# A decode layer on one core: projections as rows through four column tiles, K loads in pairs, and an attention loop without a prologue

## The chip, the cores and the metric

The kernel runs on one core of one Trainium2 chip, the chip's other cores idle. The metric is the device time of one execution in microseconds (us), the median of several runs.

In the text PE is the tensor engine, DVE the vector engine, ACT the scalar engine and "the stream" is the sequence of loads from device memory into on-chip memory. A "slot" is one of ten on-chip buffers of 16 KB a partition (2 MB) into which all large loads go.

## The reference

One token passes through one transformer layer: modulation from a condition vector, attention with 32 query heads over a cache of 4 heads x 65,536 keys, then a gated feed-forward.

```python
def reference(A_x, A_k_cache, A_v_cache, A_wq, A_wo, B_x, B_w_gate, B_w_up, B_w_down, c, w_mod):
    mod = (silu(c) @ w_mod)                 # 1024 -> 6 x 1024: sa, ca, ga, sb, cb, gb
    h = layernorm(x) * (1 + ca) + sa
    x = x + ga * attention(h)               # wq 1024x4096, caches 4x65536x128, wo 4096x1024
    h = layernorm(x) * (1 + cb) + sb
    x = x + gb * ((gelu(h @ w_gate) * (h @ w_up)) @ w_down)   # F = 3584
    return x
```

All weights and caches are bf16. The bytes are w_mod 12.6 MB, wq 8.4, the caches 134.2, wo 8.4, gate, up and w_down 7.3 each: 185.6 MB, each byte used once.

## The kernel before

The parts that the change touches. Loads are planned in the order in which they are issued, and a load waits until the previous job in its slot has been used:

```python
        wmod_v = w_mod.rearrange("(k p) n -> p k n", p=P)
        wq_v = A_wq.rearrange("(k p) n -> p k n", p=P)
        wo_v = A_wo.rearrange("(p k) n -> p k n", p=P)
        wg_v = B_w_gate.rearrange("(k p) n -> p k n", p=P)
        # ... cut
        for i in range(NC + 2):
            if i < NC:
                j_k[i] = plan_load(kv_src(kh, i), kv_view, i % SITES, kfill[i % SITES])
            if i >= 2:
                j = i - 2
                j_v[j] = plan_load(kv_src(vh, j), kv_view, SITES + j % SITES, vfill[j % SITES])
        tail = iter([8, 9, 0, 1, 2, 4, 3, 5, 6, 7, 8, 9] + [0, 1, 2, 4, 3, 5, 6, 7])
        j_o = [(plan_load(wo_v[:, k:k + 8, :], flat(8, D), next(tail)), k, 8) for k in range(0, HQ, 8)]
        # ... gate, up, w_down the same way
```

Each projection keeps a 128x128 tile of the weights stationary and streams one column, the vector. The result comes out as a column and needs no turning:

```python
                for kk in range(nk):
                    for j in range(nblk):
                        w = pick(view, kk, j) if pick else view[:, kk, j * P:(j + 1) * P]
                        ins = pe.matmul(
                            bank[:, j:j + 1], w, rhs[:, k0 + kk:k0 + kk + 1],
                            start=first, stop=True, skip_group_check=True,
                        )
```

The attention goes through 32 chunks of 64 keys a partition (2 MB of K and 2 MB of V each). PE transposes a K chunk, multiplies it with q, DVE and ACT do the softmax pieces, and PE multiplies with V two steps later (called PV). Four steps are written out, the other 28 run in a loop of four steps:

```python
        for i in range(FIRST):
            pe_step(i)
            others_step(i)
        with nc.Fori(it0, it1, engines=OrderedEngineSet([pe.engine]), head_slot={pe.engine: 0}) as it:
            # ... cut
```

Ahead of the ten slots a number of small tensors are allocated; in this kernel the slots begin at byte 62,208 of each partition.

## Time and profile before

| | before |
|---|---|
| median time | 442.9 us (442.8 to 443.1) |
| span of the profiled run | 441.7 us |
| loaded | 186.08 MB, of which 185.61 by the load queue |
| load queue's share of the 16 DMA engines | 98.8% |
| PE busy | 75% |

The page of the kernel before: first the busy time of each engine, then the DMA queues with packets, MB and share of the 16 engines' span.

```profile
PE 332.8 (75%) x7849; PEld 322.9 (73%) x7849; DVE 164.9 (37%) x282; ACT 143.1 (32%) x548; POOL 3.8 (1%) x21
...
DMA packets 15537, 186.08 MB, mean 421 GB/s; under 512 B 1553, under 2 KB 1553, under 8 KB 3985
...
q1 hardware_dynamic: 15472, 185.61, 98.8%
q8 instruction: 25, 0.41, 0.3%
```

The number to read is 98.8%: the engines that load are hardly ever idle between the first and the last load. The windows view of the same kernel says it stretch by stretch. Its columns are the stretch, then busy time and count of each engine, then the granted PE clock, the DMA share and GB/s.

```profile
5.00:60.00 55.00, 20.91 (x657) 19.92 (x658) 2.24 (x15) 0.18 (x1) 0.56 (x1) 1.00 1.01 427
60.00:110.00 50.00, 43.93 (x963) 42.28 (x962) 27.38 (x36) 20.58 (x70) 0.00 (x0) 0.91 1.01 428
110.00:360.00 250.00, 226.47 (x5006) 221.38 (x5007) 123.83 (x191) 113.36 (x442) 0.00 (x0) 0.80 1.01 431
360.00:433.00 73.00, 37.94 (x1128) 36.28 (x1124) 10.67 (x37) 7.65 (x35) 0.56 (x1) 0.53 1.01 425
```

427, 428, 431, 425 GB/s: no stretch has a gap. The Trainium skill, "DMA: Bandwidth & Descriptors", section "Where 436 GB/s comes from", gives 435.2 GB/s as the ceiling of the fabric; this trace lies 1 to 2% below it. So the time is about the bytes over the rate, plus about 2 us before the stream runs and 5.3 us after it. The end of the stream is read from the timeline of PE (start, duration, line, instruction group; in brackets how long the engine idled and what ended it):

```profile
417.37 2.02 PE L316 MATMUL kt_ps<-h_col,slot 128*128 128x1 bf16 x56 [2.31 <-DMA slot<-in_B_w_up_dram]
421.62 2.02 PE L316 MATMUL kt_ps<-h_col,slot 128*128 128x1 bf16 x56 [2.23 <-DMA slot<-in_B_w_up_dram]
426.71 1.84 PE L316 MATMUL kt_ps<-u_col,slot 128*128 128x1 bf16 x64 [3.06 <-DMA slot<-in_B_w_down_dram]
431.48 1.87 PE L316 MATMUL kt_ps<-u_col,slot 128*128 128x1 bf16 x64 [2.93 <-DMA slot<-in_B_w_down_dram]
436.37 2.86 PE L316 MATMUL kt_ps<-u_col,slot 128*128 128x1 bf16 x96 [3.02 <-DMA slot<-in_B_w_down_dram]
```

Each block costs about 2 us of matmuls and is waited for 2.2 to 3.1 us. PE would be done long before the data.

### The profile page before, as it was taken

Reading aid. Unit: us, or ns where it says so; the run is one execution under the profiler, and the core shown is the slowest. Engines: PE = TensorE matmul, PEld = TensorE weight load, DVE = VectorE, ACT = ScalarE, POOL = GpSimd, SP = SyncE. Lnnn points to the kernel's source line nnn. Section 1 sums busy time; section 2 is a strip of 40 time slices with the busy share of each in tenths; the row PEclk is TensorE's granted clock in tenths of the full one; section 3 lists DMA queues with packets and bytes.
Section 4 is the critical chain, followed back from the end, with each engine's and each line's share of the span. In section 5 each row is a group of like instructions: output and inputs, shape, how many; then the busy total and the mean of one; then the engine's idle time right before and its main releaser. Section 6 shows DMA issues by size and latency. Waiting matters only on the chain.

```text
span 441.7 us, 16769 instructions
## 1 busy us (share of the span) xinstructions
PE 332.8 (75%) x7849; PEld 322.9 (73%) x7849; DVE 164.9 (37%) x282; ACT 143.1 (32%) x548; POOL 3.8 (1%) x21
## 2 busy tenths in 40 slices
PE   2333468888989898898899898897989894463534
PEld 1333468878989798798898798787989794463534
DVE  1000036544545455444536445364454442310000
ACT  1000014444554344455443346353435353000000
POOL 2000000000000000000000000000000000000000
PEclk9999999987768969777959869699597785555555
DMA  8999999999999999999999999999999999999995
GB/s 330 428 423 426 437 427 429 426 430 422 432 426 432 432 433 429 430 429 435 430 433 430 430 429 434 429 433 431 430 429 435 428 435 429 420 424 425 426 425 213
DMA packets 15537, 186.08 MB, mean 421 GB/s; under 512 B 1553, under 2 KB 1553, under 8 KB 3985
## 3 DMA queue, kind: packets, MB, share of 16 engines
q1 hardware_dynamic: 15472, 185.61, 98.8%
q8 instruction: 25, 0.41, 0.3%
q14 instruction: 8, 0.06, 0.0%
q10 hardware_dynamic: 32, 0.00, 0.0%
HBM read 185.60 MB, written 0.00 MB: 420 GB/s over the span
## 4 chain that ended last, share of the span: by engine, by line
DMA 81%; PE 17%; issue 1%; SPq 1%; DVE 0%
DMA slot<-in_A_v_cache_dram 53%; DMA slot<-in_B_w_gate_dram 9%; PE kt_ps L417 9%; DMA slot<-in_A_k_cache_dram 8%; DMA slot<-in_B_w_down_dram 7%; DMA slot<-in_w_mod_dram 5%; PE b L481 4%; PE sc_ps L437 3%; PE kt_ps L316 1%; SPq L212 1%; PE b L451 0%; PE b L461 0%; DVE kt_sb L516 0%; PE b L668 0%; DVE y_row L670 0%
## 5 line engine op out<-in xcount | busy, mean ns | idle before, releaser
L417 PE MATMUL kt_ps<-ident,slot 128*128 128x128 bf16 x2048 | 170.1, 250 | 6.9 <-DMA slot<-in_A_k_cache_dram 3.2
L516 DVE COPY kt_sb<-kt_ps 128x2048 bf16<-128x2048 bf16 x96 | 117.6, 1225 | 102.2 <-PE kt_ps L417 102.1
L417 PEld LDWEIGHTS kt_ps<-ident,slot 128*128 128x128 bf16 x2048 | 147.5, 114 | 8.6 <-issue 7.2
L516 ACT ACTIVATE kt_sb<-kt_ps 128x2048 bf16<-128x2048 bf16 x32 | 60.1, 1877 | 219.9 <-PE kt_ps L417 219.9
L481 PE MATMUL b<-p_sb,slot 128*128 128x8 bf16 x2048 | 71.0, 167 | 29.4 <-DMA slot<-in_A_v_cache_dram 22.5
L481 PEld LDWEIGHTS b<-p_sb,slot 128*128 128x128 bf16 x2048 | 65.0, 100 | 32.2 <-DMA slot<-in_A_v_cache_dram 23.9
L547 ACT ACTIVATE p_sb<-sc_ps,mneg 128x64 bf16<-128x64 f32 x256 | 83.6, 560 | 4.2 <-DVE mneg L542 4.2
L547 ACT ACTIVATION_READ_ACCUMULATOR p_sb<-sc_ps,mneg 128x1 f32 x256 | 77.2, 364 | 0.0
L437 PE MATMUL sc_ps<-q_buf,kt_sb 128*128 128x8 bf16 x2048 | 67.1, 167 | 1.1 <-issue 1.1
L437 PEld LDWEIGHTS sc_ps<-q_buf,kt_sb 128*128 128x128 bf16 x2048 | 64.3, 99 | 1.3 <-issue 1.2
L316 PE MATMUL kt_ps<-h_col,slot 128*128 128x1 bf16 x448 | 16.2, 172 | 16.2 <-DMA slot<-in_B_w_up_dram 9.1
L316 PEld LDWEIGHTS kt_ps<-h_col,slot 128*128 128x128 bf16 x448 | 15.5, 118 | 16.9 <-DMA slot<-in_B_w_up_dram 9.5
L535 DVE TENSOR_REDUCE m_col<-sc_ps 128x8 f32<-128x512 f32 x32 | 21.8, 681 | 4.4 <-PE sc_ps L437 4.4
L316 PE MATMUL sc_ps<-s_col,slot 128*128 128x1 bf16 x384 | 11.5, 165 | 15.7 <-DMA slot<-in_w_mod_dram 15.7
L316 PEld LDWEIGHTS sc_ps<-s_col,slot 128*128 128x128 bf16 x384 | 11.0, 105 | 16.3 <-DMA slot<-in_w_mod_dram 16.3
L540 DVE TENSOR_REDUCE mg<-b 8x1 f32<-8x128 f32 x32 | 8.9, 279 | 34.8 <-PE b L451 34.8
L316 PE MATMUL sc_ps<-h_col,slot 128*128 128x1 bf16 x256 | 7.4, 165 | 12.5 <-DMA slot<-in_A_wq_dram 12.5
L316 PEld LDWEIGHTS sc_ps<-h_col,slot 128*128 128x128 bf16 x256 | 7.1, 104 | 12.8 <-DMA slot<-in_A_wq_dram 9.2
L461 PE MATMUL b<-negi,mg 8*128 8x8 f32 x64 | 14.8, 301 | 0.4 <-DVE mg L540 0.4
L461 PEld LDWEIGHTS b<-negi,mg 8*128 8x128 f32 x64 | 11.8, 229 | 2.7 <-DVE mg L540 0.6
L316 PE MATMUL kt_ps<-u_col,slot 128*128 128x1 bf16 x224 | 6.6, 165 | 9.0 <-DMA slot<-in_B_w_down_dram 9.0
L316 PEld LDWEIGHTS kt_ps<-u_col,slot 128*128 128x128 bf16 x224 | 6.3, 104 | 9.3 <-DMA slot<-in_B_w_down_dram 6.1
(74 smaller groups left out, 62.9 us busy)
## 6 DMA issues: line engine op xcount, KB each, us to landing
slot<-in_A_k_cache_dram SPq DMA_DIRECT2D x32, 2048.0 KB, 29.5
slot<-in_A_v_cache_dram SPq DMA_DIRECT2D x32, 2048.0 KB, 33.3
slot<-in_w_mod_dram SPq DMA_DIRECT2D x8, 1536.0 KB, 18.9
slot<-in_A_wq_dram SPq DMA_DIRECT2D x4, 2048.0 KB, 37.2
slot<-in_A_wo_dram SPq DMA_DIRECT2D x4, 2048.0 KB, 36.7
slot<-in_B_w_gate_dram SPq DMA_DIRECT2D x4, 1792.0 KB, 39.1
slot<-in_B_w_up_dram SPq DMA_DIRECT2D x4, 1792.0 KB, 29.1
slot<-in_B_w_down_dram SPq DMA_DIRECT2D x3, 2048.0 KB, 30.2
```

What stands on the lines that cost most here:

```text
L212: sp.dma_start(j.view, j.src).then_inc(j.tok[0], 16)
L316: ins = pe.matmul(bank[:, j:j + 1], w, rhs[:, k0 + kk:k0 + kk + 1], start=first, stop=True, skip_group_check=True,)
L417: ins = pe.transpose(kt_ps[:, half * 2048 + t * P:half * 2048 + (t + 1) * P], j_k[i].view[:, b * TB + t, :], ident[:, :],)
L437: ins = pe.matmul(sc_ps[:, base + n * REP:base + (n + 1) * REP], kt_sb[:, j % 2, n, :], q_buf[:, j % SITES, :], start=True, stop=True,)
L461: ins = pe.matmul(b6[:, 256:256 + REP], mg8[:, j % 2:j % 2 + 1].to_broadcast([REP, P]), negi[:, :], start=True, stop=True,)
L481: ins = pe.matmul(b7[:, s * REP:(s + 1) * REP], j_v[j].view[:, n, :], p_sb[:, s, n, :], start=(n == 0), stop=(n == CH - 1),)
L516: ev[i % SITES][b].done(act.activation(dst, src, ACT.Copy) if E_ is AC else dve.tensor_copy(dst, src))
L535: m1[s].done(dve.tensor_reduce(m_col[:, j % 2, :].unsqueeze(2), scv, AX.X, ALU.max))
L540: m2[s].done(dve.tensor_reduce(mg8[:, j % 2:j % 2 + 1], b6[0:REP, 32:32 + P], AX.X, ALU.max))
L547: ins = act.activation(p_sb[:, s, :, h], scv[:, h, :], ACT.Exp, bias=mneg[:, j, h:h + 1], scale=scale, accum_out=z_all[:, j, h:h + 1],)
```

## The change

The intent is to take work off PE and to make loads longer. Five things change together:

1. All projections but w_down keep the vector stationary, padded to 32 columns of which one is used, and stream rows of 512 weights. Four such matmuls use the four column tiles of the PE array. The results come out as rows, which are copied, turned by f32 transposes and gathered.
2. The weights' rows are split over partitions so that both rows of a wq, gate or up block are contiguous, and K is loaded two chunks at a time: packets of 32 KB for K, 16 for wq, 14 for gate and up, in place of 16, 8 and 7.
3. Half of wo is loaded early, after the fourth K chunk, into slots that were idle during the attention.
4. c and x are loaded with eight elements a partition (c in place of its load by rows, x in addition to it): two loads of 128 packets of 16 bytes.
5. The loop starts at step 0, with semaphores counted up in advance and zeroed tiles for the steps that do not exist.

```diff
+KU = 2
+ROW = 512
+QD = 32
...
+        act.dma_start(c_in[:, :], c[0].rearrange("(p k) -> p k", p=P)).then_inc(c_sem, 16)
+        act.dma_start(x_in[:, :], A_x[0, 0].rearrange("(p k) -> p k", p=P)).then_inc(x_sem, 16)
...
-        wq_v = A_wq.rearrange("(k p) n -> p k n", p=P)
+        wq_v = A_wq.rearrange("(p k) n -> p k n", p=P)
...
+            if i == SITES:
+                j_o = [plan_o(k) for k in range(0, 16, 8)]
+            if i < NC and i % KU == 0:
+                j_k[i] = plan_load(kv_src(kh, i, KU), flat(KU * CH, DH), i % SITES, kfill[i % SITES // KU], KU)
...
+        def row_matvec(place, jobs, pad, ready, last_k, between=None):
...
+                    for out, c0 in place(k):
+                        ins = pe.matmul(
+                            out, pad[:, k, :], jb.view[:, kk, c0:c0 + ROW],
+                            start=k <= last_k[0], stop=k >= last_k[1], skip_group_check=True,
+                        )
...
+        def quad(bank, g):
+            return kt_fp[QD * g:QD * (g + 1), bank * ROW:(bank + 1) * ROW]
...
+            for i, a in enumerate(cols):
+                ins = pe.transpose(dst[:, i * w:i * w + n], src[:, a], identf[0:src.shape[0], 0:n])
...
-        for i in range(FIRST):
-            pe_step(i)
-            others_step(i)
...
+        with nc.Fori(0, NC // SITES, engines=OrderedEngineSet([pe.engine]), head_slot={pe.engine: 0}) as it:
...
-    slots = [nc.alloc_sbuf_tensor(f"slot{i}", [P, SLOT], dt.bfloat16) for i in range(NSLOT)]
+    slot_all = nc.alloc_sbuf_tensor("slots", [P, NSLOT * SLOT], dt.bfloat16)
+    slots = [slot_all[:, i * SLOT:(i + 1) * SLOT] for i in range(NSLOT)]
```

Because other small tensors are now allocated ahead of them, the slots begin at byte 65,088 in place of 62,208. Nothing in the diff says so.

## The prediction

> **What bounds the kernel now.** The DMA stream. The page gives 186.08 MB over a 441.7 us span and the load queue 98.8% of the 16 engines' time. The windows view shows 420 to 449 GB/s in almost every stretch from 5 to 433 us (429 to 432 GB/s in the attention), never a gap. The Trainium skill ("DMA: Bandwidth & Descriptors", "Where 436 GB/s comes from") puts the fabric at 435.2 GB/s; this trace is within 1 to 2% of it. Outside the stream lie about 2 us at the start and 5.3 us at the end (timeline: 96 last matmuls from 436.37, then short steps and the store).
>
> PE is busy 75% but follows the data: the waits view charges 22.5 us to V loads, and each w_gate or w_up block takes 2.0 us of matmuls in a 4.3 us arrival interval.
>
> **What the change does.**
> 1. PE: the one-column matmuls of the mod, q, wo, gate and up projections (384+256+256+448, about 30 to 36 ns each in the timeline) become 336 matmuls of 512 columns on four column tiles. The trace has no such matmul. From the transposes (128 columns in 57 ns warm, 108 cold) I estimate 0.22 us warm, 0.43 cold each; four overlapping give about 5 us for gate, 5 for up, 9 for wo. The skill ("TensorE: Matmul & The Clock Gate", "Part 3: Packing small matmuls") reports 2.38x for three column tiles; no run here shows it yet. Saves some 6 us, off the critical path.
> 2. Added: evacuating rows (about 0.65 us), eight f32 turns (about 0.25 us each, from the trace's f32 weight load), gathers: about 3 us after wo, gate and up each, so 9 to 10 us of serial chain.
> 3. Loads: K in 4 MB pairs (32 KB a row), wq, gate and up with both rows contiguous. wq blocks land 4.90 us apart, KV blocks of equal size 4.86: about 5 ns a packet, so about 1.1 us saved. Fewer instructions to fetch (-0.4 us), two small loads of 128 tiny packets each (+0.6 us).
> 4. Half of wo (4.2 MB, 9.8 us of stream) moves ahead of the fifth K chunk. The attention therefore ends about 12 to 15 us later (before: last PV 374.3; expected 386 to 389).
>
> **Critical path.** From the last PV the serial chain is about 6.6 (combine) + 9 (wo) + 3 + 3.3 (norm) + 5 + 3 + 5 + 3 + 6.7 (w_down) + 2.4 = 47 us, so 435 at the earliest, against the stream's end at about 436 plus 5.3. Some 6 us of slack are left where there were some 17. The time stays that of the bytes.
>
> **Prediction: 442.0 us, 80% range 439.5 to 446.5.** Faster by over 2%: 1%; within 2%: 90%; slower: 9%.
>
> **Right if:** bytes unchanged, stream at 425 to 433 GB/s to about 434 us, last w_down block at about 435 and still waited for by PE; last PV at 386 to 389; K interval slightly shorter.
>
> **Wrong if:** column tiles don't overlap (gate and up then 12 us or more each at a cold clock: the chain passes the stream and the end comes at 450 to 461); DMA share drops below 0.95 after 400 us because w_down's slots come free late; K pairs leave too few loads queued and gaps appear in the attention; or 32 KB packets run nearer 435 GB/s (then 438 to 440).

## The result, and the profile after

The changed kernel takes 443.4 us (443.3 to 443.6, six runs) against 442.9 (442.8 to 443.1, six runs). The ratio is 1.0011, interval 0.9998 to 1.0024: the same time. Ratios in this text are the mean time of one kernel's fast runs over that of the other's in the same rounds, so not quite the ratio of the medians quoted. Their intervals are about 0.13% either way, some 0.6 us: a difference smaller than that, between kernels timed on different chips, is weak evidence by itself.

| | before | after |
|---|---|---|
| median time | 442.9 us | 443.4 us |
| loaded | 186.08 MB | 185.89 MB |
| packets of the load queue | 15,472 | 11,632 |
| last w_down wait ends | 436.37 us | 436.66 us |
| last PV ends | 374.3 us | 389.3 us |
| PE instructions | 7,849 | 7,107 |

The lines of the page after that answer to those above:

```profile
PE 351.4 (80%) x7107; PEld 316.9 (72%) x7107; DVE 176.2 (40%) x300; ACT 146.5 (33%) x553; POOL 11.7 (3%) x25
...
DMA packets 11957, 185.89 MB, mean 421 GB/s; under 512 B 1568, under 2 KB 1568, under 8 KB 1952
...
q1 hardware_dynamic: 11632, 185.61, 98.7%
q8 instruction: 13, 0.21, 0.2%
```

The same bytes, a quarter fewer packets, half the instruction fetches, and the queue is as full as before. PE's busy time did not fall: 351.4 us against 332.8, at a mean granted clock of 0.740 against 0.789. By this measure the intent to take work off PE was not met; PE does not set the time here. The windows of the changed kernel:

```profile
5.00:60.00 55.00, 28.31 (x203) 11.69 (x203) 10.40 (x24) 1.71 (x3) 7.27 (x2) 0.64 1.01 427
60.00:110.00 50.00, 42.69 (x907) 41.97 (x907) 21.07 (x26) 15.15 (x52) 0.00 (x0) 0.74 1.00 426
110.00:360.00 250.00, 229.15 (x5014) 223.99 (x5010) 124.03 (x194) 114.00 (x441) 0.00 (x0) 0.78 1.00 430
360.00:433.00 73.00, 47.41 (x876) 36.00 (x877) 19.90 (x54) 14.28 (x59) 0.55 (x1) 0.68 1.01 424
```

The stream was to be slightly faster in the attention, where K comes in packets twice as long. It is 430 in place of 431 GB/s. The prediction held as a whole, but a gain of about one microsecond that it counted on is not there. The timeline of PE after shows the last PV (before, it ran from 372.46 for 1.84 us), the projections and the end:

```profile
387.49 1.85 PE L625 MATMUL b<-p_sb,slots 128*128 128x8 bf16 x64 [2.96 <-ACT p_sb L691]
...
396.28 5.30 PE L392 MATMUL kt_ps<-slots,o_pad 128*32 128x512 bf16 x64 [0.39 <-DVE o_pad L766]
...
402.40 1.16 PE L453 MATMUL sc_ps<-identf,kt_sb 128*128 128x128 f32 x8 [0.82 <-DVE kt_sb L774]
...
406.94 5.08 PE L392 MATMUL kt_ps<-slots,h_pad 128*32 128x512 bf16 x56 [1.10 <-DVE h_pad L447]
...
417.45 1.04 PE L392 MATMUL kt_ps<-slots,h_pad 128*32 128x512 bf16 x14 [1.60 <-DMA slots<-in_B_w_up_dram]
421.76 1.89 PE L392 MATMUL kt_ps<-slots,h_pad 128*32 128x512 bf16 x14 [3.26 <-DMA slots<-in_B_w_up_dram]
...
426.82 1.85 PE L372 MATMUL b<-u_col,slots 128*128 128x1 bf16 x64 [0.61 <-DMA slots<-in_B_w_down_dram]
431.73 1.86 PE L372 MATMUL b<-u_col,slots 128*128 128x1 bf16 x64 [3.06 <-DMA slots<-in_B_w_down_dram]
436.66 2.94 PE L372 MATMUL b<-u_col,slots 128*128 128x1 bf16 x96 [3.07 <-DMA slots<-in_B_w_down_dram]
```

PE still waits for the last up blocks and for every w_down load, so the chain of compute does not set the end. The column tiles do overlap: 64 matmuls of 512 columns in 5.30 us are 83 ns each. At the start of that group four matmuls start within 0.02 us of each other and the next four 0.43 us later (at its end 0.22 us later), so four matmuls share the 0.43 us that the Trainium skill ("TensorE: Matmul & The Clock Gate", section "Back-to-back issue gap") gives a single one at the cold clock (N/1.2 ns, 427 for 512 columns). No run here times such matmuls on one tile alone.

### The profile page after: what moved, and what is told of

Its sections match the earlier page's. It is cut to its first block, busy times and chain, and to the rows that moved or that the text cites. A ratio compares the mean times of both kernels' runs of the same rounds, so it can differ in the third digit from the quotient of the medians.

```text
span 442.0 us, 15336 instructions
## 1 busy us (share of the span) xinstructions
PE 351.4 (80%) x7107; PEld 316.9 (72%) x7107; DVE 176.2 (40%) x300; ACT 146.5 (33%) x553; POOL 11.7 (3%) x25
## 2 busy tenths in 40 slices
DMA packets 11957, 185.89 MB, mean 421 GB/s; under 512 B 1568, under 2 KB 1568, under 8 KB 1952
## 3 DMA queue, kind: packets, MB, share of 16 engines
q1 hardware_dynamic: 11632, 185.61, 98.7%
## 4 chain that ended last, share of the span: by engine, by line
DMA 62%; PE 33%; issue 1%; DVE 1%; SPq 1%; ACT 1%
DMA slots<-in_A_v_cache_dram 39%; PE kt_ps L561 18%; DMA slots<-in_A_k_cache_dram 10%; PE b L625 7%; PE sc_ps L581 6%; DMA slots<-in_B_w_down_dram 6%; DMA slots<-in_B_w_up_dram 4%; DMA slots<-in_w_mod_dram 4%; PE b L605 1%; SPq L234 1%; PE kt_ps L392 1%; ACT p_sb L691 1%; PE b L595 1%; DVE kt_sb L751 0%; PE b L760 0%
## 5 line engine op out<-in xcount | busy, mean ns | idle before, releaser
L561 PE MATMUL kt_ps<-ident,slots 128*128 128x128 bf16 x2048 | 178.0, 257 | 11.0 <-DMA slots<-in_A_k_cache_dram 10.0
L561 PEld LDWEIGHTS kt_ps<-ident,slots 128*128 128x128 bf16 x2048 | 153.8, 117 | 12.8 <-issue 8.7
L625 PE MATMUL b<-p_sb,slots 128*128 128x8 bf16 x2176 | 75.7, 167 | 25.0 <-DMA slots<-in_A_v_cache_dram 16.1
L625 PEld LDWEIGHTS b<-p_sb,slots 128*128 128x128 bf16 x2176 | 69.5, 100 | 27.9 <-DMA slots<-in_A_v_cache_dram 17.3
L392 PE MATMUL kt_ps<-slots,h_pad 128*32 128x512 bf16 x176 | 17.5, 526 | 13.1 <-DMA slots<-in_A_wq_dram 6.4
L392 PEld LDWEIGHTS kt_ps<-slots,h_pad 128*32 128x32 bf16 x176 | 5.3, 117 | 23.0 <-DMA slots<-in_A_wq_dram 8.3
L392 PE MATMUL kt_ps<-slots,s_pad 128*32 128x512 bf16 x96 | 13.6, 588 | 8.7 <-DMA slots<-in_w_mod_dram 8.7
L453 PEld LDWEIGHTS sc_ps<-identf,kt_sb 128*128 128x128 f32 (+1 forms) x48 | 7.6, 204 | 8.2 <-DVE kt_sb L774 4.3
L453 PE MATMUL sc_ps<-identf,kt_sb 128*128 128x128 f32 (+1 forms) x48 | 9.1, 352 | 4.5 <-DVE kt_sb L774 2.4
L372 PE MATMUL b<-u_col,slots 128*128 128x1 bf16 x224 | 6.6, 165 | 6.8 <-DMA slots<-in_B_w_down_dram 6.7
```

Source lines behind the costliest of these rows:

```text
L372: ins = pe.matmul(bank[:, j:j + 1], view[:, kk, j * P:(j + 1) * P], rhs[:, k0 + kk:k0 + kk + 1], start=first, stop=True, skip_group_check= ...
L392: ins = pe.matmul(out, pad[:, k, :], jb.view[:, kk, c0:c0 + ROW], start=k <= last_k[0], stop=k >= last_k[1], skip_group_check=True,)
L453: ins = pe.transpose(dst[:, i * w:i * w + n], src[:, a], identf[0:src.shape[0], 0:n])
L561: ins = pe.transpose(kt_ps[:, half * 2048 + t * P:half * 2048 + (t + 1) * P], j_k[i - i % KU].view[:, i % KU * CH + b * TB + t, :], ident[ ...
L625: ins = pe.matmul(b7[:, s * REP:(s + 1) * REP], j_v[j].view[:, n, :], p_sb[:, s, n, :], start=(n == 0), stop=(n == CH - 1),)
```

## The experiments

The first question was where the microsecond of the longer packets went. The theory from the prediction (A) is that each packet costs about 5 ns and something else took the gain back; the rivals are that packet length does not matter (B) or that long K packets are themselves slower (C). Each group of four kernels ran on one chip with the kernel before beside it; that kernel took 442.9, 443.25 and 443.2 us in the three groups, so differences are taken within a group or by ratio.

### k_single: K in single chunks

```diff
-KU = 2
+KU = 1
```

> The changed kernel with K again in single chunks (2 MB loads, 16 KB packets); all else as changed. Theory A (as predicted: each packet costs about 5 ns, and the gain of the longer packets was eaten by something else): +0.6 us against the changed kernel, 444.0 us. Theory B (the stream runs at a rate per byte that packet length does not change): 443.4 us, within 0.2. Theory C (the long K packets or their lumpy order are themselves slightly slower; the cycle of eight KV chunks took 39.0 us against 38.9): back to 442.8 us.

444.6 us, ratio 1.0041 (1.0028 to 1.0054), against 1.0011 for the changed kernel. The single chunks cost 1.2 us. That falls on A's side, at twice its size: 2,048 more packets are 128 on each of 16 engines, so 1.2 us is about 9 ns a packet, not 5. B and C are out. The trace confirms the packet count (13,936 in place of 11,632 on the load queue, 256 of the difference being the semaphore writes of 16 more loads).

### short_packets: gate and up in packets of 7 KB

```diff
+    def gap(n):
+        return lambda t: t.rearrange("p (k n) -> p k n", k=2)[:, :, 0:n]
...
-        j_g = [(plan_load(wg_v[:, k:k + 2, :], flat(2, F), next(tail)), k, 2) for k in range(0, KD, 2)]
+        j_g = [(plan_load(wg_v[:, k:k + 2, :], gap(F), next(tail)), k, 2) for k in range(0, KD, 2)]
```

(and the same for up)

> The changed kernel with gate and up rows kept 512 elements apart on chip, so that their loads go in packets of 7 KB as before in place of 14 KB (1,024 packets more length for length; same bytes). Theory A (5 ns a packet): +0.3 us, 443.7. Theory B (packet length does not matter here): 443.4 within 0.1; blocks of up still land 4.3 us apart.

444.1 us, ratio 1.0027 (1.0014 to 1.0040): +0.64 us against the changed kernel. 1,024 more packets are 64 an engine, so 10 ns each. Two ways of adding packets agree at 9 to 10 ns. (The intervals of the two ratios overlap; the single runs, 443.9 to 444.2 against 443.3 to 443.6 us, do not.) The expectation's 5 ns came from the trace of the kernel before. Why does a packet cost twice as much in the changed kernel as it seemed to cost in the old one? That question led to theory D below.

### small_loads: the two loads of 16-byte packets, added to the kernel before

```diff
+        act.dma_start(c_in[:, :], c[0].rearrange("(p k) -> p k", p=P)).then_inc(xtra, 16)
+        act.dma_start(x_in[:, :], A_x[0, 0].rearrange("(p k) -> p k", p=P)).then_inc(xtra, 16)
```

> The kernel before with the two added loads of 128 packets of 16 bytes (c and x by partition), not used by anything. If these small packets cost the stream about 0.6 us as I estimated: 443.5 us. If they are free: 442.9 within 0.1.

443.7 us, ratio 1.0019 (1.0006 to 1.0032): +0.8 us. The two loads carry 4 KB in 256 packets, 16 an engine. The estimate of 0.6 was nearly right, but the time is not explained as a cost by packet. The trace file keeps the start, size and duration of every packet (the packet records; the views print only their sums): a packet of 16 bytes took 8.5 ns, so the 16 of an engine took 0.14 us. In the profiled run, 0.4 us slower than the kernel before, the stream is 0.3 us behind once 0.5 MB have landed and stays 0.2 to 0.4 us behind. The changed kernel, which has the same two loads, is not behind at that point (0.5 MB after 3.93 us, 4.13 in the kernel before). So this +0.8 us need not hold there.

### wo_late: half of wo not loaded early

```diff
             if i == SITES:
-                j_o = [plan_o(k) for k in range(0, 16, 8)]
+                pass
...
-        j_o += [plan_o(k) for k in range(16, HQ, 8)]
+        j_o += [plan_o(k) for k in range(0, HQ, 8)]
```

> The changed kernel with all of wo loaded after the caches, as before; K stays in pairs. If the stream alone sets the time: no change, 443.4 us within 0.3, while the last PV moves from 389 back to about 379 (it gives the 9.8 us of early wo back). If the early wo load costs something of the half microsecond lost: 442.9.

445.6 us (445.2 to 448.1), ratio 1.0080 (1.0061 to 1.0098). Neither expectation was right: it is 2.2 us slower by the medians. The windows view of wo_late shows why:

```profile
95.00:100.00 5.00, 5.00 (x123) 5.00 (x121) 3.28 (x4) 1.38 (x10) 0.00 (x0) 0.73 1.01 429
100.00:105.00 5.00, 4.81 (x117) 4.68 (x114) 2.64 (x5) 3.67 (x14) 0.00 (x0) 1.00 0.81 295
105.00:110.00 5.00, 4.68 (x144) 4.61 (x142) 3.29 (x6) 1.31 (x7) 0.00 (x0) 1.00 0.98 421
```

For once the DMA share drops to 0.81 and the rate to 295 GB/s. Its timeline shows the next K pair issued only at 101.33 us, when PE has finished with the pair in its slots. With K in pairs the queue holds fewer loads that may start, and in the first steps of the attention, where PE is behind (its granted clock is 0.50 from 85 to 95 us), it runs dry. The changed kernel covers that hole with the 4.2 MB of wo: there the same stretch has 393 GB/s. So the early wo is not an extra: here it fills a hole of about 2 us. That the pairs make the hole, and not the loop without a prologue, is argued: no run has single chunks and all of wo late in the changed kernel.

### slots_256: slots on a 256-byte boundary

Theory D: it matters where in a partition a load lands. The slots of the kernel before start at 62,208 = 243 x 256. Those of the changed kernel start at 65,088 = 254 x 256 + 64. Two tensors of 32 bytes a partition, moved behind the slots, put them at 65,024 = 254 x 256:

```diff
-    att_nat = sb("att_nat", [P, KD])
-    x1_nat = sb("x1_nat", [P, KD])
...
     slots = [slot_all[:, i * SLOT:(i + 1) * SLOT] for i in range(NSLOT)]
+    att_nat = sb("att_nat", [P, KD])
+    x1_nat = sb("x1_nat", [P, KD])
```

> The changed kernel with two small tensors allocated after the load slots in place of ahead of them, so that the slots start at byte 65,024 of a partition (a multiple of 256) in place of 65,088 (64 over a multiple of 256). Nothing else differs. Theory D (a packet whose destination is not on a 256-byte boundary costs the DMA engines a few ns more; before's slots are on such boundaries, the changed kernel's are not): about 4 ns for each of some 650 packets an engine, 2.6 us, so 441 us, below both kernels. Rival E (placement is nothing, the missing 2 us went into the queue's order or the row pitch of the weights): 443.4 within 0.2.

440.5 us (440.3 to 440.5), ratio 0.9939 (0.9925 to 0.9952). Set against the changed kernel's ratio of 1.0011 this is 0.72%, 3.2 us by ratio (2.9 by the medians). The best version is the changed kernel with two lines moved. In its PE timeline the end comes 3.0 us earlier, and the rhythm of the w_down loads is 4.84 and 4.85 us where it was 4.91 and 4.93. The windows show a higher rate at the same DMA share; first two stretches of the changed kernel, then the same two of slots_256, then the end of its timeline:

```profile
10.00:60.00 50.00, 28.31 (x203) 11.69 (x203) 6.39 (x21) 1.61 (x2) 2.27 (x2) 0.61 1.01 430
60.00:110.00 50.00, 42.69 (x907) 41.97 (x907) 21.07 (x26) 15.15 (x52) 0.00 (x0) 0.74 1.00 426
...
10.00:60.00 50.00, 26.82 (x203) 11.38 (x203) 6.37 (x21) 1.61 (x2) 2.25 (x2) 0.63 1.01 433
60.00:110.00 50.00, 40.79 (x913) 40.04 (x914) 21.20 (x26) 15.25 (x52) 0.00 (x0) 0.77 1.01 430
...
423.97 1.84 PE L372 MATMUL b<-u_col,slots 128*128 128x1 bf16 x64 [0.49 <-DVE u_col L841]
428.81 1.87 PE L372 MATMUL b<-u_col,slots 128*128 128x1 bf16 x64 [3.00 <-DMA slots<-in_B_w_down_dram]
433.66 2.89 PE L372 MATMUL b<-u_col,slots 128*128 128x1 bf16 x96 [2.98 <-DMA slots<-in_B_w_down_dram]
```

### before_off64 and before_off128: the kernel before, pushed off the boundary

```diff
+    off = sb("off", [P, 16])        # 64 bytes; 32 for 128 bytes
     slots = [nc.alloc_sbuf_tensor(f"slot{i}", [P, SLOT], dt.bfloat16) for i in range(NSLOT)]
```

> The kernel before with an unused tensor of 64 bytes a partition ahead of the slots: they start 64 bytes over a multiple of 256. Theory D: some 870 packets an engine at about 4 ns, +3.5 us, 446.4 us. Rival E: 442.9 within 0.2.

447.2 us, ratio 1.0089 (1.0074 to 1.0105): +3.9 us. From 110 to 360 us the rate is 428 GB/s in place of 431:

```profile
110.00:360.00 250.00, 224.46 (x4995) 219.20 (x4993) 123.71 (x193) 114.34 (x442) 0.00 (x0) 0.81 1.01 428
```

> The same with 128 bytes: slots 128 over a multiple of 256. If the boundary that matters is 256 bytes: like the 64-byte shift (446.4). If it is 128 or 64 lines: 442.9. Rival E: 442.9.

446.8 us, ratio 1.0082 (1.0068 to 1.0096): +3.6 us. So an offset of 128 bytes is as bad as one of 64, and since the slots of the kernel before start at an odd multiple of 256, no boundary wider than 256 is needed. Rival E, for which placement is nothing, is out: an unused tensor costs the old kernel almost 1%. The kernel before has 13,952 data packets (its 15,472 less 16 semaphore writes for each of 95 loads and stores), 872 an engine; 3.6 to 3.9 us are 4.1 to 4.5 ns a packet.

### k_single_256: both together

The edit is slots_256 with `KU = 1`.

> The changed kernel with slots on 256-byte boundaries and K in single chunks. Against slots_256 (440.5) it has 128 more packets an engine. At 5 ns a packet: 441.1; at 9 to 10 ns, as the off-boundary runs showed: 441.7. Against k_single (444.6) it shows the boundary again: 776 packets an engine at 4.5 ns would be 3.5 us (441.1), a cost by bytes alone would be 2.9 (441.7).

441.1 us, ratio 0.9955 (0.9941 to 0.9968). Against slots_256 (0.9939) that is +0.65 us for 128 packets an engine: 5.1 ns. Against k_single (444.6) it is -3.5 us by the medians for 776 packets: 4.5 ns. By these times a packet costs about 5 ns when its destination starts on the boundary and about 9.5 ns when it does not. That the cost goes by packet and not by byte is not shown by the times: the same bytes in more packets lose more (3.5 us here against 2.9 in the pair version by the medians, 3.8 against 3.2 by ratio), but the difference is within the intervals, and rests on four kernels timed on three chips.

The packet records of the kept traces show it. Mean duration of a packet of the load queue (768 to 5,120 packets each):

| packet | on the boundary | 64 bytes off it | difference |
|---|---|---|---|
| 7 KB | 273.0 ns (before) | 277.2 ns (before_off64) | 4.2 |
| 8 KB | 310.0 (slots_256) | 315.0 (after) | 5.0 |
| 14 KB | 536.5 (slots_256) | 541.6 (after) | 5.1 |
| 16 KB | 611.9 (slots_256) | 615.7 (after) | 3.8 |
| 32 KB | 1,213.9 (slots_256) | 1,217.7 (after) | 3.8 |

A packet of 32 KB loses no more than one of 7 KB: 4 to 5 ns a packet, whatever its length. (The 12 KB packets of w_mod vary too much to tell.) Two packets of 16 KB take 10 ns longer than one of 32 on the boundary, and 14 ns off it. The times show some 5 ns less of each; the records of packets overlap in part, by 3.2 us an engine in k_single_256 and 2.6 in slots_256, and that difference is 4 to 5 ns for each added packet.

### tile_runs: matmuls sorted by column tile

```diff
-                for kk in range(nk):
-                    k = k0 + kk
-                    for out, c0 in place(k):
+                todo = [(out, c0, k0 + kk, kk) for kk in range(nk) for out, c0 in place(k0 + kk)]
+                todo.sort(key=lambda a: quad_of[id(a[0])])
+                for out, c0, k, kk in todo:
```

(`quad_of` remembers the tile of each output.)

> The changed kernel with each block's matmuls of 512 columns sorted by column tile, so that up to four in a row use the same tile; same work, right result. If tiles overlap only between neighbours in program order: wo 5.3 to about 13 us, gate 5.1 to about 12, the last up block 1.9 to about 5; the serial chain then passes the stream and the end comes at about 454 us. If the PE overlaps them whatever the order: 443.4.

443.3 us, ratio 1.0004 (0.9988 to 1.0019). The PE timeline of this kernel:

```profile
393.36 5.58 PE L392 MATMUL kt_ps<-slots,o_pad 128*32 128x512 bf16 x64 [0.39 <-DVE o_pad L771]
...
404.32 5.22 PE L392 MATMUL kt_ps<-slots,h_pad 128*32 128x512 bf16 x56 [1.10 <-DVE h_pad L452]
```

5.58 us in place of 5.30, and 5.22 in place of 5.08. Four in a row on one tile hardly matter. In this trace, too, four matmuls start together every 0.43 us, so PE must have started matmuls of other tiles ahead of earlier ones of the same tile (the trace does not name the tile). Ends of matmuls in a trace are modelled, but the copy on DVE that needs the 64 starts at 399.03 us, so the 5.6 us are real. Started strictly in order, the 16 matmuls of each of the four loads would take 12 steps, each of the 0.22 us or more seen between two rounds: over 10 us in all. This run did not show what happens if tiles never overlap, since they always did.

### half_gu_before and half_gu_after: 7.34 MB less to load

Only one of the two rows of each gate and up block is loaded and used twice; the result is wrong, the work on PE is the same.

```diff
-        j_g = [(plan_load(wg_v[:, k:k + 2, :], flat(2, F), next(tail)), k, 2) for k in range(0, KD, 2)]
+        j_g = [(twice(plan_load(wg_v[:, k:k + 1, :], flat(1, F), next(tail))), k, 2) for k in range(0, KD, 2)]
```

(and the same for up; `twice` lets both rows read the one that was loaded)

> Wrong result on purpose. The kernel before with only one of the two rows of each gate and up block loaded and used for both: 7.34 MB less to load, the same work on PE. At 429 GB/s that is 17.1 us of stream. The serial chain after the attention should end well before the shorter stream, so if the stream sets the time: 425.8 us. If something else does: less than 17 us gained.

426.3 us: 17.0 us gained (443.2 to 426.3) where the bytes over the rate give 17.1. In the kernel before, the time is the bytes. (1,024 packets go with them; this run does not tell the two apart.)

> Wrong result on purpose. The same cut of 7.34 MB in the changed kernel. If its serial chain has the slack I now read from its trace (some 12 us between where the chain could end and where it ends): chain-bound at about 431 us, 12 us gained in place of 17. If my predicted slack of 6 us was right: about 437. If the chain does not bind at all: 426.3.

430.2 us, with unsteady runs from 427.4 to 432.5: about 13 us gained against the changed kernel's 443.4, not 17. In its profiled run PE no longer waits for weights after the attention; the chain runs through, and by windows the DMA share is 0.39 from 420 to 425 us:

```profile
420.00:425.00 5.00, 4.37 (x171) 4.30 (x168) 0.00 (x0) 0.00 (x0) 0.00 (x0) 0.76 0.39 149
```

Last PV to last instruction: 388.45 to 428.1, 39.7 us. That is the length of the serial chain that I had put at 47.

### down_split: a smaller load near the end

slots_256 with the third w_down load split in two loads of one block.

```diff
-        while b + 2 < NBF:
+        while b + 3 < NBF:
...
-            for e, ne in ((0, 2), (2, 1), (3, 1)):
+            for e, ne in ((0, 2), (2, 1), (3, 1)) if b == NBF - 1 else ((0, UE),):
```

> slots_256 with the third w_down load (2 MB, two blocks) split in two of 1 MB. Its 64 matmuls then don't all stand behind its slowest landing, so of the 96 matmuls (2.9 us) after the last wait about 32 move ahead of it: about -1 us, 439.5. If the last landing is the later small loads' anyway: no change, 440.5.

440.4 us, ratio 0.9936: no change against slots_256. The 2.9 us of matmuls at the end do not hang on that one landing: the last group of 96 came apart into 32, 32, 24 and 8, but the last 8 wait for a load until 436.22 us and end at 436.6, where the 96 of slots_256 end too. So the end follows the last landing.

## Why the prediction was right or wrong

**Right: the time is the bytes.** 442.0 was predicted with 439.5 to 446.5, 443.4 was measured. half_gu_before shows it directly: 17.0 us for 7.34 MB. That the number came within 1.4 us is partly luck: the sum lacked a loss of some 3 us (the placement, below), and more than 1.5 us of gain beyond the 0.9 that it counted on, and the two misses had opposite signs. Of the marks under "Right if" two were narrowly missed: the last w_down wait ended at 436.66, not about 435, and eight K and V chunks took 39.0 us, not less than the 38.9 before.

**Right: the projections' saving is off the critical path, and four column tiles overlap.** The term for wo was mis-sized: 9 us estimated, 5.3 measured. I had let the two matmuls that follow each other on one tile wait for one another; tile_runs shows that their order hardly matters.

**Right: the attention ends 12 to 15 us later.** The last PV ends at 389.3, 0.3 us past the 386 to 389 expected. I had counted this as a harmless shift of bytes. wo_late shows that it is more: without the early wo a hole of about 2 us opens near 100 us. The prediction named such gaps as a risk of the K pairs, and did not see that the early wo was there to fill them.

**Wrong in size: the slack of the serial chain.** "Some 6 us of slack" was too little: 47 us of chain were estimated, 39.7 run in half_gu_after, so the slack is about 13 us (389.3 + 39.7 = 429.0 against 442.0). wo at 5.3 and not 9, the turns at about 2 us and not 3, and the up projection at 3.6 us when its data is there, and not 5, make the difference. It did not bind either way.

**Right in size: about 5 ns a packet.** k_single_256 against slots_256 gives 5.1 ns, and with it the 1.1 us expected for 3,584 fewer data packets (224 an engine). But it holds only on the boundary. (Its source, blocks 0.04 us further apart for 8 more packets an engine, is too coarse to tell 5 ns from 4 or 6.)

**Missing: the term that took it back.** Step 3 summed longer packets (-1.1), fewer instructions (-0.4) and small loads (+0.6) to about -0.9 us. The sum lacked the placement of the slots, 64 bytes off a 256-byte boundary: +2.9 us by the medians, +3.2 by ratio, shown by slots_256 and, in the other direction, by both shifted versions of the kernel before. So "442.0" came out 1.4 us low. The change contains a real gain: in the same rounds slots_256 is 0.61% faster than the kernel before. An accident of allocation hid it.

**Open.** The terms that were measured do not add up fully. From the kernel before to slots_256 the medians give -2.8 us in the same rounds. Packets (-1.1) and small loads (+0.8) leave -2.5, and no experiment tests what that is. The packet records of the two traces narrow it. The 16 engines finish less evenly in the kernel before (DMA share 0.56, 0.50 and 0.52 from 435 to 438 us) than in slots_256 (0.62, 0.42 and 0.27 from 433 to 436, then nothing): slots_256 is 2.1 us ahead when 184 of the 185.6 MB have landed and 2.7 at the end, so this is worth about 0.6 us. The packets of the instruction queue take 0.75 us an engine in place of 1.45, some 0.7 less. And the +0.8 of the small loads is not seen at the start of slots_256. With -1.1 for the packets that makes about -2.4 of the -2.8. What made the end even is not tested; nor was the new row pitch of the weights tested by itself.

## What to carry to other kernels

When a kernel is bound by its loads, look at where the destinations start on chip, not only at how long the packets are: here 64 bytes of padding were worth 0.7 to 0.9%, and an innocent tensor allocated ahead of the buffers decided it. Pad large load buffers to 256 bytes before comparing two kernels whose small tensors differ; otherwise the comparison measures the allocation. And when a change moves loads about, ask what was filling the queue at each moment: the pairs of K without the early wo left a hole of 2 us.

## What the Trainium skill lacked or had wrong

- "DMA: Bandwidth & Descriptors", section "How a descriptor splits into AXI transactions", tells that a read starting off a 256-byte boundary costs extra beats. It says nothing of where a load's destination starts on chip. Here destinations 64 or 128 bytes off cost 4 to 5 ns a packet for packets of 7 to 32 KB: 2.9 us of 443 in one kernel, 3.6 to 3.9 in the other. The runs do not show the mechanism.
- The same page, section "Why small descriptors are slow (HBM only)", gives a fixed overhead of about 3 cycles a packet and weighs it for a packet of 256 bytes alone. Here packets of 16 KB in place of 32 KB for K still cost 0.65 us of 441: 5.1 ns a packet on the boundary, 9 to 10 ns off it.
- "TensorE: Matmul & The Clock Gate", "Part 3: Packing small matmuls", reports 2.38x for three column tiles and calls matmuls strictly in order in start and end. Here four column tiles with 512 columns run four in 0.43 us at the cold clock, the time of one, and sorting them so that up to four in a row use one tile changes 64 of them only from 5.30 to 5.58 us, which strict order would not allow (over 10 us, worked out at tile_runs).
